# S and DP formed as rows in four column groups, and wider wq transfers, in a one-core attention and MLP gradient kernel

## Chip, cores and metric

The kernel runs on one NeuronCore of a Trainium2 chip. The core has a matrix engine (TensorE, PE in the profile; its weight loads are shown apart as PEld), a vector engine (DVE), an activation engine (ACT), GpSimd (POOL) and a queue engine (SP) that here issues nearly all transfers. The transfers themselves run on 16 DMA engines. Each engine works through its own queue in order; engines wait for each other through semaphores. The metric is the device time of one execution in microseconds (us), lower is better.

## Reference

One decode step and all its gradients. An attention block with 32 heads reads one query row against a cache of 4096 keys and values a head; a small MLP runs beside it, and a gate mixes the two. Cut to what matters:

```python
q = (x @ wq).reshape(32, 128)
scores = einsum("hd,hkd->hk", q, k_cache) * 128 ** -0.5
p = softmax(scores)
o = einsum("hk,hkd->hd", p, v_cache)
a = o.reshape(4096) @ wo
b = mish(x @ w1 + b1) @ w2
out = g * a + (1 - g) * b            # g = sigmoid(x . gate_w)
# returned: out, and the gradients of x, k_cache, v_cache, wq, wo, w1, b1, w2, gate_w
```

The caches are 32 x 4096 x 128 in bf16, so K and V are read once (2 x 33.6 MB) and dK and dV written once (the same). For a head, S is the row of 4096 scores. DP is the row of 4096 products of V with dO, the gradient of o for that head. p is softmax(S), and ds = p * (DP - D) with one number D a head. dV is the outer product of p and dO, dK that of ds and q.

## The kernel before

**Tiling.** The 4096 keys of a head lie as 128 partitions x J = 32 keys x 128 numbers, 1 MB (`Kn`, four buffers, and `Vn`, three). S and DP are kept as 128 partitions x 32, the same layout, in PSUM. The 32 heads run one after the other in groups of G = 4 heads; a group shares 512 columns of wq (`wq_p`, one transfer of 1.3 MB for two groups, in runs of 2048 B) and 512 rows of wo (`wo_g`).

**One head.** The order in the source is the order in each engine's queue. For head h:

- `v_tr` (four blocks, `tr_block`, L514 and L515): PE transposes V as f32 words into the PSUM tile `tr` (two buffers), ACT copies each block of 512 columns to `VT`. Between the blocks stand `dqo_mm` (L624), four f32 products of the head before on the weights `od_sb`, and `softmax` (L548, L550), which turns the diagonal `dgm` of the partition maxima into the head's maximum `negM`.
- `dk_out(h - 1)` (L581): DVE forms dK of the head before in the buffer `o_sb` (two instructions of 128 x 2048), and SP issues its store (L591).
- `exps` (L556): ACT takes the exponentials of S. `dP` (L522): PE forms DP with `cols_mm`, then DVE multiplies DP with them (`pj`, L562).
- `k_tr(h + 1)`: K of the next head is transposed to `KT` in four blocks, with `zd_mm` (L566, the sums over partitions of the exponentials and of `pj`) after the second block. DVE then makes p and ds (`probs`, L570 to L576) and dV (`dv_out`, L581).
- `scores(h + 1)`: S of the next head with `cols_mm` (L522), DVE takes its maximum over the 32 columns (`m`, L542), ACT makes `dgm` (L544).
- `dq_o` (L611): 16 products in four column groups of PE, K with ds and V with p, 512 columns each, into `od4`; `od_cp` (L618) copies it to `od_sb` on ACT.

`cols_mm` uses the transposed keys as weights: for each of 16 words and two halves of a word it loads 128 x 128 bf16 weights from T and multiplies them with a 32-column slice of `qz` (for S) or `doz` (for DP), a tile in which q or dO of the head stands in two columns between zeros. So S and DP take 32 weight loads and 32 products each, all summed in one 128 x 32 tile. T is one of `KT` and `VT`, one buffer each.

**Group work.** Around the heads of a group stand the steps for the neighbours: `g_q`, `g_do`, `g_dodiag`, `g_dobc`, `g_docol`, `g_dopair` prepare q and dO of the next group (`pair_cp`, L235, writes `qz` and `doz` in two DVE instructions), `f_diag`, `f_bc`, `f_dx`, `f_dwq`, `f_dwo` finish the gradients of the group before, `mlp_some` and `dw2_some` spread the MLP over the heads. `load_wqp` is called at the end of groups 0, 2 and 4 (and once at the start), `f_dwq_st` stores dwq after every second group.

**Queues.** SP issues loads and stores in program order: `load_k(h + 4)` and `load_v(h + 3)` after `od_cp(h)`, each store after its producer. The last stores are dV and dK of head 31 (L591), behind the small outputs `fin_rows`.

Of the kernel before, what the change touches and what calls it, by code (L numbers as in the profile page):

```python
# [16 lines left out]
def kernel(  # L17
# [24 lines left out]
    nc = tc.nc  # L42
# [71 lines left out]

    wqp = {}

    def load_wqp(k):
        wqp[k] = wts.tile([P, RC, 2 * GD], BF16, name="wq_p", tag="wq_p", bufs=2)
        for i in range(2):
            wqs[2 * k + i] = wqp[k][:, :, i * GD:(i + 1) * GD]  # L120
        nc.sync.dma_start(wqp[k][:], wq_v[:, :, 2 * k * GD:2 * (k + 1) * GD])

    def load_wo(g):
        wos[g] = wts.tile([P, G, D], BF16, name="wo_g", tag="wo_g")
# [58 lines left out]
    dx_parts = const.tile([P, RC, NG + 3], F32, name="dx_parts")  # L183

    p4b, ds4b = [], []
    qz = const.tile([P, G, 3 * J - 2], BF16, name="qz")
    doz = const.tile([P, G, 3 * J - 2], BF16, name="doz")
    nc.gpsimd.memset(qz[:], 0.0)
    nc.gpsimd.memset(doz[:], 0.0)
    for i in range(3):  # L190
        for lst, nm in ((p4b, "p4"), (ds4b, "ds4")):
            lst.append(const.tile([P, J * 4], BF16, name=f"{nm}{i}"))
# [3 lines left out]

    def g_new(g):
        groups[g] = dict(
            q_row=grp_sb.tile([P, GD], BF16, name="q_row", tag="q_row"),
            qs_row=grp_sb.tile([P, GD], BF16, name="qs_row", tag="qs_row"),  # L200
            do_row=grp_sb.tile([P, GD], BF16, name="do_row", tag="do_row"),
            do_col=grp_sb.tile([P, G], F32, name="do_col", tag="do_col"),
            dqo=grp_sb.tile([P, 2, G], F32, name="dqo", tag="dqo"),
        )
# [26 lines left out]
        return ps  # L231

    def pair_cp(z, ps):
        for par in range(2):
            nc.vector.tensor_tensor(z[:, :, J - 2 + par * J:J + par * J],  # L235
                                    ps[:, par, :].unsqueeze(2).to_broadcast([P, G, 2]),
                                    half[:].unsqueeze(1).to_broadcast([P, G, 2]), ALU.mult)

    def g_qcol(g):
        groups[g]["col"] = col_mm(groups[g]["q_row"])  # L240
# [13 lines left out]
    def g_do(g, hh):  # L254
        gp = groups[g]
        junk = small.tile([P, D], BF16, name="junk", tag="junk", bufs=1)
        nc.vector.scalar_tensor_tensor(junk[:], in0=wos[g][:, hh, :], scalar=1.0, in1=da_bc[:],  # L257
                                       op0=ALU.mult, op1=ALU.mult, accum_out=gp["do_col"][:, hh:hh + 1])

    def g_diag(src, sc, a, b):  # L260
        diag = grp_sb.tile([P, G, P], BF16, name="diag", tag="diag")
# [21 lines left out]
    def f_new(g):  # L283
        gp = groups[g]
        gp["o_bf"] = grp_sb.tile([P, G], BF16, name="o_bf", tag="o_bf")
        gp["dq_bc"] = grp_sb.tile([P, GD], BF16, name="dq_bc", tag="dq_bc")

    def f_diag(g, a=0, b=G):
        gp = groups[g]
# [87 lines left out]
        nc.vector.tensor_scalar(wqs[g][:, c, cs], groups[g]["dq_bc"][:, cs], x_col_f[:, c:c + 1], None, ALU.mult)  # L377

    def f_dwq_st(g):
        if g % 2:  # L380
            k = g // 2
            nc.sync.dma_start(dwq_v[:, :, 2 * k * GD:2 * (k + 1) * GD], wqp[k][:])

    def f_dwo(g, hh):
        nc.scalar.activation(wos[g][:, hh, :], da_bc[:], ACT.Copy, scale=groups[g]["o4"][:, hh:hh + 1])  # L385
# [124 lines left out]
    def tr_block(src, dst, c):  # L510
        tp = tr_ps.tile([P, TB // 2, P], F32, name="tr", tag="tr")
        words = src[:, c * TB:(c + 1) * TB, :].rearrange("p a b -> p (a b)").bitcast(F32)
        for t in range(TB // 2):
            nc.tensor.transpose(tp[:, t, :], words[:, t * P:(t + 1) * P], ident_f[:])  # L514
        nc.scalar.copy(dst[:, c * (TB // 2):(c + 1) * (TB // 2), :], tp[:])  # L515

    def cols_mm(out, T, z):
        Tb = T[:].rearrange("p c r -> p (c r)").bitcast(BF16).rearrange("p (c r a) -> p c r a", r=P, a=2)
        for c in range(J // 2):
            for par in range(2):  # L520
                a = J - 2 - 2 * c + par * J
                nc.tensor.matmul(out, lhsT=Tb[:, c, :, par], rhs=z[:, a:a + J],  # L522
                                 start=(c == 0 and par == 0), stop=(c == J // 2 - 1 and par == 1))

    def k_tr(h, c):
        if h < H:
            if c == 0:
                KT[h] = kvT.tile([P, J // 2, P], F32, name="KT", tag="KT")
            tr_block(kts[h], KT[h], c)

    def v_tr(h, c):
        if c == 0:
            VT[h] = kvT.tile([P, J // 2, P], F32, name="VT", tag="VT")
        tr_block(vts[h], VT[h], c)

    def scores(h):
        if h >= H:
            return
        S_ps[h] = s_ps.tile([P, J], F32, name="S", tag="S")
        cols_mm(S_ps[h][:], KT.pop(h), qz[:, h % G, :])  # L540
        m32 = small.tile([P, 1], F32, name="m32", tag="m32")
        nc.vector.reduce_max(m32[:], S_ps[h][:], axis=AX.X)  # L542
        dgms[h] = small.tile([P, P], F32, name="dgm", tag="dgm", bufs=1)
        nc.scalar.activation(dgms[h][:], ident_bf[:], ACT.Copy, scale=m32[:])  # L544

# [7 lines left out]
    def exps(h, negM):  # L553
        es[h] = small.tile([P, J], BF16, name="e_bf", tag="e_bf")
        zds[h] = small.tile([P, 2], F32, name="zd", tag="zd")
        nc.scalar.activation(es[h][:], S_ps.pop(h)[:], ACT.Exp, bias=negM[:], scale=scale, accum_out=zds[h][:, 0:1])  # L556

    def dP(h):
        DP_ps[h] = s_ps.tile([P, J], F32, name="DP", tag="DP")
        cols_mm(DP_ps[h][:], VT.pop(h), doz[:, h % G, :])  # L560
        pj = small.tile([P, J], F32, name="pj", tag="pj")
        nc.vector.scalar_tensor_tensor(pj[:], in0=DP_ps[h][:], scalar=1.0, in1=es[h][:],  # L562
                                       op0=ALU.mult, op1=ALU.mult, accum_out=zds[h][:, 1:2])

    def zd_mm(h, mx):
# [2 lines left out]
    def probs(h, mx):  # L568
        rz = small.tile([P, 1], F32, name="rz", tag="rz")
        nc.vector.reciprocal(rz[:], mx[:, P:P + 1])  # L570
        negD = small.tile([P, 1], F32, name="negD", tag="negD")
        nc.vector.tensor_scalar(negD[:], mx[:, P + 1:P + 2], rz[:], -1.0, ALU.mult, ALU.mult)
        p4s[h] = p4b[h % 3][:, 0:J * 4].rearrange("p (j t) -> p j t", t=4)
        nc.vector.tensor_scalar(p4s[h], es.pop(h)[:].unsqueeze(2).to_broadcast([P, J, 4]), rz[:], None, ALU.mult)
        ds4s[h] = ds4b[h % 3][:, 0:J * 4].rearrange("p (j t) -> p j t", t=4)
        nc.vector.scalar_tensor_tensor(ds4s[h], in0=DP_ps.pop(h)[:].unsqueeze(2).to_broadcast([P, J, 4]),  # L576
                                       scalar=negD[:], in1=p4s[h], op0=ALU.add, op1=ALU.mult)
        zds.pop(h)

# [13 lines left out]
    def dv_out(h):  # L593
        out_pair(h, dVv, p4s[h], groups[h // G]["do_row"])
# [10 lines left out]
    def dq_o(h):  # L605
        K, V = kts.pop(h), vts.pop(h)
        for r in range(J // 8):
            for c in range(4):
                N, c4 = (K, ds4b[h % 3]) if c < 2 else (V, p4b[h % 3])
                jb = 4 * (2 * r + c % 2)  # L610
                nc.tensor.matmul(od4[32 * c:32 * c + 4, :],  # L611
                                 lhsT=c4[:, 4 * jb:4 * jb + 16].rearrange("p (j t) -> p t j", t=4)[:, 0, :],
                                 rhs=N[:, jb:jb + 4, :].rearrange("p j d -> p (j d)"),
                                 start=(r == 0), stop=(r == J // 8 - 1))

    def od_cp(h):
        od_sb[h] = small.tile([P, 4, Dh], F32, name="od_sb", tag="od_sb", bufs=1)
        nc.scalar.copy(od_sb[h][:].rearrange("p j d -> p (j d)"), od4[:])  # L618

    def dqo_mm(h):  # L620
# [90 lines left out]
    for h in range(H - 1):  # L711
# [206 lines left out]
```

## Time and profile before

| | |
|---|---|
| median of 3 runs | 407.63 us (407.42 to 408.31) |
| profiled execution | 409.23 us, its span in the profile 407.4 us |
| moved by DMA | 164.76 MB, 404 GB/s on average |
| wq_p load | 4 transfers of 1280 KB |
| dwq store | 4 transfers of 1280 KB |
| K load, V load, dK and dV store | 32, 32 and 64 transfers of 1024 KB |
| weight loads of L522 | 2 x 1024, 100 and 97 ns |
| products of L522 | 2 x 1024, 180 and 177 ns, overlapping |
| o_sb, L581 | 128 instructions, 1217 ns each |
| ACT copies of T, L515 | 256, 585 and 588 ns each |

The page shows one execution taken by the hardware profiler, times in us unless marked ns. "Busy" is the time in which an engine had work in it; PE's matrix products are pipelined, so single products overlap and their ends are modelled. The rows of 40 digits cut the span in 40 slices and give the busy share of each in tenths; PEclk is the share of the full clock that PE was granted, DMA the mean share of the 16 DMA engines. The chain that ended last goes back from the last instruction, at each step to what released it. A line of a timeline gives the start, the time from the first to the last of the merged instructions, engine, source line, operation, the tile written and read, the count, and in brackets idle time before it with its releaser. In a line of waits stand the total, the number of waits and the longest. A line of stretches gives its length, then for PE, PEld, DVE, ACT and POOL the busy time and number of instructions, then the granted clock, the DMA share and GB/s.

### The profile page before, as it was taken

Reading aid. Unit: us, or ns where it says so; the run is one execution under the profiler, and the core shown is the slowest. Engines: PE = TensorE matmul, PEld = TensorE weight load, DVE = VectorE, ACT = ScalarE, POOL = GpSimd, SP = SyncE. Lnnn points to the kernel's source line nnn. Section 1 sums busy time; section 2 is a strip of 40 time slices with the busy share of each in tenths; the row PEclk is TensorE's granted clock in tenths of the full one; section 3 lists DMA queues with packets and bytes.
Section 4 is the critical chain, followed back from the end, with each engine's and each line's share of the span. In section 5 each row is a group of like instructions: output and inputs, shape, how many; then the busy total and the mean of one; then the engine's idle time right before and its main releaser. Section 6 shows DMA issues by size and latency. Waiting matters only on the chain.

```text
span 407.4 us, 10856 instructions
## 1 busy us (share of the span) xinstructions
PE 332.7 (82%) x4445; PEld 271.9 (67%) x4445; DVE 306.6 (75%) x845; ACT 232.6 (57%) x479; POOL 10.0 (2%) x25
## 2 busy tenths in 40 slices
PE   2698998889898998989898898879989798989600
PEld 1487776677686977877677678758777676877500
DVE  3646774797898587998999785666899987995640
ACT  2345556666476453765567666765776553776520
POOL 3000001000000000000000003000000000000000
PEclk9989999989898597999999896787999987899755
DMA  8999999999999999999999999999999999999883
GB/s 290 427 415 422 416 414 404 403 420 421 417 421 423 422 419 421 414 426 421 424 424 425 426 418 425 416 426 422 424 408 405 426 417 425 422 386 421 359 333 133
DMA packets 28695, 164.76 MB, mean 404 GB/s; under 512 B 2916, under 2 KB 3045, under 8 KB 12262
## 3 DMA queue, kind: packets, MB, share of 16 engines
q1 hardware_dynamic: 28338, 164.05, 97.8%
q8 instruction: 35, 0.57, 0.5%
q14 instruction: 14, 0.11, 0.1%
q0 software_dynamic: 256, 0.01, 0.0%
q10 hardware_dynamic: 52, 0.01, 0.0%
HBM read 82.03 MB, written 82.03 MB: 403 GB/s over the span
## 4 chain that ended last, share of the span: by engine, by line
DVE 44%; PE 34%; ACT 10%; issue 5%; DMA 2%; DVEq 0%; ACTq 0%; SPq 0%
DVE o_sb L581 22%; PE tr L514 15%; PE dqo_ps L624 7%; DVE junk L327 3%; PE DP L522 3%; ACT od_sb L618 2%; DVE junk L257 2%; DVE ds L576 2%; DMA wq_p<-in_A_wq_dram 2%; PE q_ps L210 2%; PE od L611 2%; PE mx L548 2%; ACT KT L515 2%; ACT VT L515 2%; ACT wo_g L385 2%
## 5 line engine op out<-in xcount | busy, mean ns | idle before, releaser
L515 ACT COPY VT<-tr 128x512 f32<-128x512 f32 x128 | 72.6, 585 | 43.3 <-PE tr L514 41.4
L514 PE MATMUL tr<-ident_f,Vn 128*128 128x128 f32 x512 | 90.2, 314 | 3.4 <-ACT VT L515 1.8
L515 ACT COPY KT<-tr 128x512 f32<-128x512 f32 x128 | 69.8, 588 | 39.4 <-PE tr L514 38.7
L514 PE MATMUL tr<-ident_f,Kn 128*128 128x128 f32 x512 | 78.6, 301 | 8.7 <-DMA Kn<-in_A_k_cache_dram 5.9
L514 PEld LDWEIGHTS tr<-ident_f,Vn 128*128 128x128 f32 x512 | 69.1, 166 | 15.0 <-ACT VT L515 7.3
L581 DVE TENSOR_TENSOR o_sb<-qs_row,ds 128x2048 bf16<-128x2048 bf16 x64 | 75.2, 1217 | 0.3 <-DMA out_dram<-o_sb 0.3
L581 DVE TENSOR_TENSOR o_sb<-do_row,p 128x2048 bf16<-128x2048 bf16 x64 | 75.2, 1217 | 0.0
L514 PEld LDWEIGHTS tr<-ident_f,Kn 128*128 128x128 f32 x512 | 61.3, 154 | 13.6 <-DVE ident_f L165 5.8
L544 ACT ACTIVATE dgm<-ident_bf,m 128x128 f32<-128x128 bf16 x32 | 12.8, 401 | 57.8 <-DVE m L542 48.6
L550 DVE TENSOR_REDUCE negM<-mx 128x1 f32<-128x128 f32 x32 | 9.3, 291 | 44.8 <-PE mx L548 34.0
L624 PE MATMUL dqo_ps<-sel,od_sb 128*128 128x2 f32 x256 | 37.2, 267 | 6.8 <-ACT od_sb L618 5.1
L624 PEld LDWEIGHTS dqo_ps<-sel,od_sb 128*128 128x128 f32 x256 | 35.5, 215 | 9.7 <-ACT od_sb L618 7.3
L522 PE MATMUL DP<-doz,VT 128*128 128x32 bf16 x1024 | 37.0, 180 | 2.3
L522 PEld LDWEIGHTS <-VT 128*128 128x128 bf16 x1024 | 34.0, 100 | 6.4 <-ACT VT L515 4.3
L522 PEld LDWEIGHTS <-KT 128*128 128x128 bf16 x1024 | 32.3, 97 | 6.0 <-ACT KT L515 3.2
L522 PE MATMUL S<-qz,KT 128*128 128x32 bf16 x1024 | 34.2, 177 | 1.9
L611 PE MATMUL od<-Kn,ds 128*4 128x512 bf16 x256 | 33.3, 382 | 0.0
L611 PE MATMUL od<-Vn,p 128*4 128x512 bf16 x256 | 33.3, 382 | 0.0
L257 DVE SCALAR_TENSOR_TENSOR junk<-wo_g,da_bc 128x640 bf16<-128x640 bf16 x32 | 26.3, 820 | 0.4
L385 ACT ACTIVATE wo_g<-da_bc,o 128x640 bf16<-128x640 bf16 x32 | 24.6, 820 | 0.0
L327 DVE SCALAR_TENSOR_TENSOR junk<-wq_p,dq_bc 128x512 bf16<-128x512 bf16 x35 | 24.0, 687 | 0.5
L618 ACT COPY od_sb<-od 128x512 f32<-128x512 f32 x32 | 18.2, 568 | 1.4 <-PE od L611 1.2
(171 smaller groups left out, 337.4 us busy)
## 6 DMA issues: line engine op xcount, KB each, us to landing
out_dram<-o_sb SPq DMA_DIRECT2D x64, 1024.0 KB, 15.1
Kn<-in_A_k_cache_dram SPq DMA_DIRECT2D x32, 1024.0 KB, 17.2
Vn<-in_A_v_cache_dram SPq DMA_DIRECT2D x32, 1024.0 KB, 17.9
wq_p<-in_A_wq_dram SPq DMA_DIRECT2D x4, 1280.0 KB, 14.7
wo_g<-in_A_wo_dram SPq DMA_DIRECT2D x8, 640.0 KB, 16.9
out_dram<-wo_g SPq DMA_DIRECT2D x8, 640.0 KB, 17.5
out_dram<-wq_p SPq DMA_DIRECT2D x4, 1280.0 KB, 16.3
w_sb<-in_B_w_dram SPq DMA_DIRECT2D x1, 2160.0 KB, 23.1
```

What stands on the lines that cost most here:

```text
L257: nc.vector.scalar_tensor_tensor(junk[:], in0=wos[g][:, hh, :], scalar=1.0, in1=da_bc[:], op0=ALU.mult, op1=ALU.mult, accum_out=gp["do_col ...
L327: nc.vector.scalar_tensor_tensor(junk[:, cs], in0=wqs[g][:, c, cs], scalar=1.0, in1=gp["dq_bc"][:, cs], op0=ALU.mult, op1=ALU.mult, accum_ ...
L385: nc.scalar.activation(wos[g][:, hh, :], da_bc[:], ACT.Copy, scale=groups[g]["o4"][:, hh:hh + 1])
L514: nc.tensor.transpose(tp[:, t, :], words[:, t * P:(t + 1) * P], ident_f[:])
L515: nc.scalar.copy(dst[:, c * (TB // 2):(c + 1) * (TB // 2), :], tp[:])
L522: nc.tensor.matmul(out, lhsT=Tb[:, c, :, par], rhs=z[:, a:a + J], start=(c == 0 and par == 0), stop=(c == J // 2 - 1 and par == 1))
L544: nc.scalar.activation(dgms[h][:], ident_bf[:], ACT.Copy, scale=m32[:])
L550: nc.vector.tensor_reduce(negM[:], mx[:, 0:P], axis=AX.X, op=ALU.max, negate=True)
L581: nc.vector.tensor_tensor(dst[:, a:b, :].rearrange("p j (k t) -> p j k t", t=4), row.rearrange("p (k t) -> p k t", t=4).unsqueeze(1).to_br ...
L611: nc.tensor.matmul(od4[32 * c:32 * c + 4, :], lhsT=c4[:, 4 * jb:4 * jb + 16].rearrange("p (j t) -> p t j", t=4)[:, 0, :], rhs=N[:, jb:jb + ...
L618: nc.scalar.copy(od_sb[h][:].rearrange("p j d -> p (j d)"), od4[:])
L624: nc.tensor.matmul(od_sb[h][:], lhsT=t[:, j, :], rhs=sel[:, :, j], start=(j == 0), stop=(j == 3))
```

## The change

S and DP are formed the other way round. Now q (or dO) is the weight, two columns of it, and the transposed keys are the moving side: `rows_mm` sends 512 columns of T through each of four column groups of PE, once for each half of a word, eight products in all. The result `row4` has two rows in each group. ACT copies it to `row_sb` (128 x 512 f32), and the new `cols_mm` turns it back into the 128 x 32 layout with four f32 products against a fixed selection `sel_s`. The two parts are separate calls in the head's order: `dp_rows` before and `dP` after the first block of `k_tr(h + 1)`; `s_rows(h + 1)` before and `scores(h + 1)` after `dq_o(h)`. S and DP share one PSUM tile `sdp`.

`KT` and `VT` share one buffer; `row_sb` shares its buffer with the old `od_sb`; `q_row`, `diag` and `dq_bc` have one buffer instead of two. `qz` and `doz` shrink to two columns a head, and `pair_cp` writes them in one instruction. wq of groups 2 to 5, and dwq of them, become one transfer each of 2.6 MB in runs of 4096 B; groups 0 and 1, and 6 and 7, stay as pairs, and share one buffer.

```diff
+    WQP = [(0, 2), (2, 6), (6, NG)]
     def load_wqp(k):
-        wqp[k] = wts.tile([P, RC, 2 * GD], BF16, name="wq_p", tag="wq_p", bufs=2)
-        for i in range(2):
-            wqs[2 * k + i] = wqp[k][:, :, i * GD:(i + 1) * GD]
-        nc.sync.dma_start(wqp[k][:], wq_v[:, :, 2 * k * GD:2 * (k + 1) * GD])
+        a, z = WQP[k]
+        wqp[k] = wts.tile([P, RC, (z - a) * GD], BF16, name="wq_p", tag=f"wq_{z - a}", bufs=1)
+        for g in range(a, z):
+            wqs[g] = wqp[k][:, :, (g - a) * GD:(g - a + 1) * GD]
+        nc.sync.dma_start(wqp[k][:], wq_v[:, :, a * GD:z * GD])
...
-    qz = const.tile([P, G, 3 * J - 2], BF16, name="qz")
-    doz = const.tile([P, G, 3 * J - 2], BF16, name="doz")
-    nc.gpsimd.memset(qz[:], 0.0)
-    nc.gpsimd.memset(doz[:], 0.0)
+    qz = const.tile([P, 2, G, 2], BF16, name="qz")
+    doz = const.tile([P, 2, G, 2], BF16, name="doz")
+    sel_s = const.tile([P, 4, J], F32, name="sel_s")
+    nc.gpsimd.memset(sel_s[:], 0.0)
+    for i in range(2):
+        nc.gpsimd.affine_select(
+            out=sel_s[:], in_=sel_s[:], compare_op=ALU.not_equal, fill=1.0,
+            base=-3 * i, pattern=[[-8, 4], [4, J]], channel_multiplier=-1,
+        )
...
-            q_row=grp_sb.tile([P, GD], BF16, name="q_row", tag="q_row"),
+            q_row=grp_sb.tile([P, GD], BF16, name="q_row", tag="q_row", bufs=1),
...
     def f_dwq_st(g):
-        if g % 2:
-            k = g // 2
-            nc.sync.dma_start(dwq_v[:, :, 2 * k * GD:2 * (k + 1) * GD], wqp[k][:])
+        for k, (a, z) in enumerate(WQP):
+            if g == z - 1:
+                nc.sync.dma_start(dwq_v[:, :, a * GD:z * GD], wqp[k][:])
...
-    def cols_mm(out, T, z):
-        Tb = T[:].rearrange("p c r -> p (c r)").bitcast(BF16).rearrange("p (c r a) -> p c r a", r=P, a=2)
-        for c in range(J // 2):
-            for par in range(2):
-                a = J - 2 - 2 * c + par * J
-                nc.tensor.matmul(out, lhsT=Tb[:, c, :, par], rhs=z[:, a:a + J],
-                                 start=(c == 0 and par == 0), stop=(c == J // 2 - 1 and par == 1))
+    def rows_mm(T, z, hh):
+        Tb = T[:].rearrange("p c r -> p (c r)").bitcast(BF16).rearrange("p (g n a) -> p g n a", g=4, a=2)
+        for par in range(2):
+            for c in range(4):
+                nc.tensor.matmul(row4[32 * c:32 * c + 2, :], lhsT=z[:, par, hh, :], rhs=Tb[:, c, :, par],
+                                 start=(par == 0), stop=(par == 1))
+        row_sb = small.tile([P, 4, P], F32, name="row_sb", tag="row_sb", bufs=1)
+        nc.scalar.copy(row_sb[:].rearrange("p c r -> p (c r)"), row4[:])
+        return row_sb
+
+    def cols_mm(out, row_sb):
+        for c in range(4):
+            nc.tensor.matmul(out, lhsT=row_sb[:, c, :], rhs=sel_s[:, c, :], start=(c == 0), stop=(c == 3))
...
+    s_rows(0)
+    g_dodiag(0)
     scores(0)
-    g_dodiag(0)
...
         exps(h, negM)
+        dp_rows(h)
+        k_tr(h + 1, 0)
         dP(h)
-        k_tr(h + 1, 0)
         k_tr(h + 1, 1)
...
         dv_out(h)
+        s_rows(h + 1)
+        dq_o(h)
         scores(h + 1)
-        dq_o(h)
         od_cp(h)
...
-            if g % 2 == 0 and g + 2 < NG:
-                load_wqp(g // 2 + 1)
+            if g in (0, 4):
+                load_wqp(g // 4 + 1)
```

More of the change, by code (lines that the diff above doesn't have):

```diff
@@ L115 @@
     wqp = {}
+    WQP = [(0, 2), (2, 6), (6, NG)]
+    assert NG == 8
     def load_wqp(k):
-        wqp[k] = wts.tile([P, RC, 2 * GD], BF16, name="wq_p", tag="wq_p", bufs=2)
-        for i in range(2):
-            wqs[2 * k + i] = wqp[k][:, :, i * GD:(i + 1) * GD]
-        nc.sync.dma_start(wqp[k][:], wq_v[:, :, 2 * k * GD:2 * (k + 1) * GD])
+        a, z = WQP[k]
[3 more added lines that the diff above has]
+        nc.sync.dma_start(wqp[k][:], wq_v[:, :, a * GD:z * GD])
     def load_wo(g):
@@ L233, in pair_cp @@
     def pair_cp(z, ps):
-        for par in range(2):
-            nc.vector.tensor_tensor(z[:, :, J - 2 + par * J:J + par * J],
-                                    ps[:, par, :].unsqueeze(2).to_broadcast([P, G, 2]),
-                                    half[:].unsqueeze(1).to_broadcast([P, G, 2]), ALU.mult)
+        nc.vector.tensor_tensor(z[:].rearrange("p a h j -> p (a h) j"),
+                                ps[:].rearrange("p a h -> p (a h)").unsqueeze(2).to_broadcast([P, 2 * G, 2]),
+                                half[:].unsqueeze(1).to_broadcast([P, 2 * G, 2]), ALU.mult)
     def g_qcol(g):
@@ L260, in g_diag @@
     def g_diag(src, sc, a, b):
-        diag = grp_sb.tile([P, G, P], BF16, name="diag", tag="diag")
+        diag = grp_sb.tile([P, G, P], BF16, name="diag", tag="diag", bufs=1)
         for hh in range(a, b):
@@ L274, in g_dodiag @@
         gp = groups[g]
-        gp["do_diag"] = grp_sb.tile([P, G, P], BF16, name="diag", tag="diag")
+        gp["do_diag"] = grp_sb.tile([P, G, P], BF16, name="diag", tag="diag", bufs=1)
         nc.vector.tensor_tensor(gp["do_diag"][:].rearrange("p h d -> p (h d)").rearrange("p (k t) -> p k t", t=4),
@@ L285, in f_new @@
         gp["o_bf"] = grp_sb.tile([P, G], BF16, name="o_bf", tag="o_bf")
-        gp["dq_bc"] = grp_sb.tile([P, GD], BF16, name="dq_bc", tag="dq_bc")
+        gp["dq_bc"] = grp_sb.tile([P, GD], BF16, name="dq_bc", tag="dq_bc", bufs=1)
     def f_diag(g, a=0, b=G):
@@ L515, in tr_block @@
         nc.scalar.copy(dst[:, c * (TB // 2):(c + 1) * (TB // 2), :], tp[:])
-    def cols_mm(out, T, z):
-        Tb = T[:].rearrange("p c r -> p (c r)").bitcast(BF16).rearrange("p (c r a) -> p c r a", r=P, a=2)
-        for c in range(J // 2):
-            for par in range(2):
-                a = J - 2 - 2 * c + par * J
-                nc.tensor.matmul(out, lhsT=Tb[:, c, :, par], rhs=z[:, a:a + J],
-                                 start=(c == 0 and par == 0), stop=(c == J // 2 - 1 and par == 1))
+    row4 = s_ps.tile([P, 4 * P], F32, name="row4", tag="row4")
+    nc.vector.memset(row4[:], 0.0)
+    sdp = s_ps.tile([P, 2, J], F32, name="sdp", tag="sdp")
+    def rows_mm(T, z, hh):
[10 more added lines that the diff above has]
+            nc.tensor.matmul(out, lhsT=row_sb[:, c, :], rhs=sel_s[:, c, :], start=(c == 0), stop=(c == 3))
     def k_tr(h, c):
@@ L527, in k_tr @@
             if c == 0:
-                KT[h] = kvT.tile([P, J // 2, P], F32, name="KT", tag="KT")
+                KT[h] = kvT.tile([P, J // 2, P], F32, name="KT", tag="T")
             tr_block(kts[h], KT[h], c)
@@ L532, in v_tr, with s_rows @@
         if c == 0:
-            VT[h] = kvT.tile([P, J // 2, P], F32, name="VT", tag="VT")
+            VT[h] = kvT.tile([P, J // 2, P], F32, name="VT", tag="T")
         tr_block(vts[h], VT[h], c)
+    rows_sb = {}
+    def s_rows(h):
+        if h < H:
+            rows_sb["S"] = rows_mm(KT.pop(h), qz, h % G)
     def scores(h):
@@ L538, in scores @@
             return
-        S_ps[h] = s_ps.tile([P, J], F32, name="S", tag="S")
-        cols_mm(S_ps[h][:], KT.pop(h), qz[:, h % G, :])
+        S_ps[h] = sdp[:, 0, :]
+        cols_mm(S_ps[h], rows_sb.pop("S"))
         m32 = small.tile([P, 1], F32, name="m32", tag="m32")
-        nc.vector.reduce_max(m32[:], S_ps[h][:], axis=AX.X)
+        nc.vector.reduce_max(m32[:], S_ps[h], axis=AX.X)
         dgms[h] = small.tile([P, P], F32, name="dgm", tag="dgm", bufs=1)
@@ L555, in exps, with dp_rows @@
         zds[h] = small.tile([P, 2], F32, name="zd", tag="zd")
-        nc.scalar.activation(es[h][:], S_ps.pop(h)[:], ACT.Exp, bias=negM[:], scale=scale, accum_out=zds[h][:, 0:1])
+        nc.scalar.activation(es[h][:], S_ps.pop(h), ACT.Exp, bias=negM[:], scale=scale, accum_out=zds[h][:, 0:1])
+    def dp_rows(h):
+        rows_sb["DP"] = rows_mm(VT.pop(h), doz, h % G)
     def dP(h):
-        DP_ps[h] = s_ps.tile([P, J], F32, name="DP", tag="DP")
-        cols_mm(DP_ps[h][:], VT.pop(h), doz[:, h % G, :])
+        DP_ps[h] = sdp[:, 1, :]
+        cols_mm(DP_ps[h], rows_sb.pop("DP"))
         pj = small.tile([P, J], F32, name="pj", tag="pj")
-        nc.vector.scalar_tensor_tensor(pj[:], in0=DP_ps[h][:], scalar=1.0, in1=es[h][:],
+        nc.vector.scalar_tensor_tensor(pj[:], in0=DP_ps[h], scalar=1.0, in1=es[h][:],
                                        op0=ALU.mult, op1=ALU.mult, accum_out=zds[h][:, 1:2])
@@ L575, in probs @@
         ds4s[h] = ds4b[h % 3][:, 0:J * 4].rearrange("p (j t) -> p j t", t=4)
-        nc.vector.scalar_tensor_tensor(ds4s[h], in0=DP_ps.pop(h)[:].unsqueeze(2).to_broadcast([P, J, 4]),
+        nc.vector.scalar_tensor_tensor(ds4s[h], in0=DP_ps.pop(h).unsqueeze(2).to_broadcast([P, J, 4]),
                                        scalar=negD[:], in1=p4s[h], op0=ALU.add, op1=ALU.mult)
@@ L616, in od_cp @@
     def od_cp(h):
-        od_sb[h] = small.tile([P, 4, Dh], F32, name="od_sb", tag="od_sb", bufs=1)
+        od_sb[h] = small.tile([P, 4, Dh], F32, name="row_sb", tag="row_sb", bufs=1)
         nc.scalar.copy(od_sb[h][:].rearrange("p j d -> p (j d)"), od4[:])
@@ L831 @@
     exps(h, negM)
+    dp_rows(h)
     dP(h)
```

## Prediction

> **What bounds the kernel now.** I read the page first (busy shares, clock and DMA slices, the chain), then the waits, then the timeline of one ordinary head, then busy time by stretches.
>
> ```profile
> PE 332.7 (82%) x4445; PEld 271.9 (67%) x4445; DVE 306.6 (75%) x845; ACT 232.6 (57%) x479; POOL 10.0 (2%) x25
> ...
> PEclk9989999989898597999999896787999987899755
> DMA  8999999999999999999999999999999999999883
> ...
> q8 instruction: 35, 0.57, 0.5%
> ...
> DVE 44%; PE 34%; ACT 10%; issue 5%; DMA 2%; DVEq 0%; ACTq 0%; SPq 0%
> ```
>
> Two things look like the bound. The 16 DMA engines are nine tenths busy or more from the second slice to the third last. But the chain that ended last is 88% DVE, PE and ACT, and 2% DMA. The waits decide between them:
>
> ```profile
> ACT dgm L544 <- DVE m L542: 48.6, 25, 2.5
> ...
> DVE negM L550 <- PE mx L548: 34.0, 17, 5.5
> ...
> DVE pj L562 <- PE DP L522: 6.8, 9, 2.2
> ...
> PE tr L514 <- DMA Kn<-in_A_k_cache_dram: 5.9, 1, 5.9
> ```
>
> The one large wait for a landing is the first K. After it the compute engines wait for each other. So each head is a closed loop of work that hands over from engine to engine, and DMA keeps up because its queue was filled at the start. Head 2, from its maximum m to the next head's:
>
> ```profile
> 39.95 0.18 DVE L542 TENSOR_REDUCE m<-S 128x1 f32<-128x32 f32 x1
> ...
> 40.53 0.57 ACT L618 COPY od_sb<-od 128x512 f32<-128x512 f32 x1
> ...
> 41.15 1.05 PE L624 MATMUL dqo_ps<-sel,od_sb 128*128 128x2 f32 x8 [0.72 <-ACT od_sb L618]
> ...
> 42.74 1.92 ACT L515 COPY VT<-tr 128x512 f32<-128x512 f32 x3 [1.15 <-PE tr L514]
> ...
> 43.87 1.21 PE L522 MATMUL DP<-doz,VT 128*128 128x32 bf16 x32
> ...
> 45.50 0.18 DVE L562 SCALAR_TENSOR_TENSOR pj<-DP,e_bf 128x32 f32<-128x32 f32 x1
> ...
> 46.99 1.07 ACT L515 COPY KT<-tr 128x512 f32<-128x512 f32 x2 [0.26 <-PE tr L514]
> ...
> 47.27 1.21 PE L522 MATMUL S<-qz,KT 128*128 128x32 bf16 x32
> 47.35 2.35 DVE L581 TENSOR_TENSOR o_sb<-do_row,p 128x2048 bf16<-128x2048 bf16 x2
> ...
> 48.41 0.38 PE L611 MATMUL od<-Kn,ds 128*4 128x512 bf16 x2
> ...
> 49.62 0.18 DVE L542 TENSOR_REDUCE m<-S 128x1 f32<-128x32 f32 x1
> ```
>
> V's last copy ends at 44.66, DP at 45.08, and pj follows at 45.50. K's last copy ends at 48.06, S at 48.48, and m follows at 49.62 behind the dV product. So 24 of the 32 products of each sum run while the last copy is made, and only 0.42 us stand behind it. The loop is 9.67 us. Read the same way in the timeline, the steps from m to m of heads 0 to 30 sum to 353.3 us, 11.4 us a head with the work of the groups in it.
>
> **The change, part by part.** *DP as rows.* Removed: 32 weight loads and products. Added, behind V's last copy: two rounds of four products, a copy of 512 columns by ACT, four f32 products (sel_s). Their nearest rows: od, also four column groups of 512 columns, starts a round every 0.21 us (48.41, 48.63, 48.85, 49.06); the od_sb copy is of the same size, 0.57; dqo, four f32 products with the same kind of weights, is 1.05 and starts 0.05 behind its copy. From V's last copy: 0.15 to the fourth group's first product (as DP now), 0.21 to its second, 0.50 to the copy (in head 31 od's last round starts at 380.70 and the copy at 381.20), 0.57 copy, 0.05, 1.05: DP ends 2.53 us behind V's copy instead of 0.42. pj follows 0.11 behind DP at the least; over heads 0 to 30 it now starts 0.45 behind on average. So pj comes 2.53 + 0.11 - 0.43 - 0.45 = 1.76 us later, 55 us over 31 heads; heads 14 and 26, whose pj is 1.2 and 2.2 us behind DP anyway, take less: 53. Queued behind: on ACT the copy stands ahead of K's four copies, and on PE sel_s's products ahead of K's second block of transposes. Following that queue, K's last copy ends 5.13 us behind V's instead of 3.40, which is the same 1.73, so both ways round the loop move together. zd then waits for that second block, 0.05 a head: 1.6.
>
> *S as rows.* The same detour behind K's last copy, but od's 16 products stand between rows and sel_s: 0.15 + 0.21 + four rounds of 0.21, 0.32 until the next work starts behind od's last round (49.06 to 49.38), 1.05: S ends 2.6 behind K's copy instead of 0.44. m now starts 1.16 behind S on average, 0.11 at the least: 2.6 + 0.11 - 0.44 - 1.16 = 1.11 a head, 34 over 31. What waits for m is dgm on ACT, od_sb queued behind it there, then dqo and mx on PE, negM and dK on DVE: nothing that could hide it. Head 31 has only the DP detour: 2.
>
> PE also stands still 0.32 us behind od's last round, where it goes from four column groups back to whole products. DP as rows brings two more such changes a head, 0.64 us; both lie inside the wait for ACT's copy (0.50 + 0.57), so I count nothing.
>
> *Unknown prices.* Rows read T two bytes out of four, which no product here does as the moving side: a round between 0.21 (od) and 0.42 (twice od's), 0 to 26 us over 62 detours with two rounds each; I take 0.21, since the weight loads of L522 read T with that step now, 100 ns, and those of L269's ones without one are 100 ns too. The f32 products are 32 columns wide: between 0.6 (a block of four f32 transposes) and 1.2 (DP's 32 products); I take dqo's 1.05, the same weights. The low end takes away 28 us, the high end adds 9.
>
> *Transfers.* wq and dwq of groups 2 to 5, 5.24 MB, go in runs of 4096 B. In the stretch 388.5 to 390.5, where mostly 2048 B runs move, DMA makes 385 GB/s, in 200 to 220, K, V and outputs, 425. So they take 13.6 us now and 12.3 at the best: 0 to 1.3, I take 0.65. PE's instructions arrive as 35 packets (q8), one for 254 of its 8890 records; it has 2048 fewer, 8 packets of 16 KB, 0.3 us. Neither counts while the loop paces; if DMA did, 1 us.
>
> *At no cost.* One buffer for q_row, diag and dq_bc: each is written at one head of four and last read a head or more before the next write. T shared by K and V: K's copy stands behind ACT's row copy, which has waited for V's rows. row_sb shared with od_sb: od_sb stands behind dgm, which needs S. Without these covers each would add up to 0.57 a head. sel_s replaces two POOL fills before 5 us and is first used after 16. One instead of two products per qz or doz: 0.12 x 16, -2.
>
> *The end.* The last o_sb is ready at 391.6, its store and the one before are issued at 394.32 and 395.07, and the span ends at 407.4. The first K, issued at 0.74, was there at 5.87, and a further 1 MB at 425 GB/s takes 2.5: two such transfers alone 7.6 us, to 401.9. The other 5 us are earlier stores that DMA is behind with, and a longer loop leaves it none: -5.
>
> Sum: 53 + 34 + 2 + 2 - 2 - 5 = +84. The profiled execution took 409.23 us (span 407.4), so 493; the runs' median is 1.6 lower: **491 us**.
>
> **Rivals.** *More half speed on PE.*
>
> ```profile
> 154.20:157.60 3.40, 1.64 (x22) 0.83 (x14) 3.37 (x7) 1.65 (x4) 0.00 (x0) 1.00 1.02 424
> 157.60:164.40 6.80, 6.76 (x62) 6.53 (x62) 4.55 (x16) 2.24 (x6) 0.00 (x0) 0.50 1.01 422
> ```
>
> A stretch with PE busy 1.64 of 3.40 us is followed by 6.8 us at clock 0.50. Heads 12, 20 and 28, each with such a stretch, take 12.7 us, heads 16 and 24 of the same kind 10.5: 2.2. Eighteen slow windows of 3.4 us between 24 and 380 cost so about 20. The loop gains some 2 us of PE idleness a head; twice the windows: 511. Against it: no single new gap exceeds 0.7 us. The Trainium skill, "TensorE: Matmul & The Clock Gate", Part 1, says that an idle window of about 3.4 us halves the clock; the trace agrees with the length, but its windows were half busy.
> *Changes between whole and grouped products unhidden*: the 0.64 us x 31 = 20 from above, 511. For it, the 0.32 us appears behind every od; against it, the copy covers it. The Trainium skill, "TensorEngine Tiling (Array Packing)", section Key Properties, says that a change of tiling mode drains TensorE, which would apply at each of them; the 0.32 us agrees, and no run here shows how much of it a wait can hide.
> *Cheaper detours.* f32 products at 0.6: 491 - 28 = 463; with the slow windows gone too, 443.
> *No overlap of the four groups.* Each round 0.84: 1.26 more a detour, 78 us, 569. od's rows, two starting at once, speak against it.
> *The other side: DMA paces.* If the heads are in truth held back by transfers, through buffers that come free late, the detours fill idle time and the transfers decide: 407.6 - 1 = 406.6. The DMA slices speak for it; the waits, the chain and the even 9.6 us of the plain heads against. It decides only while the added time a head stays under some 0.16 us, the 5 us of the end over 31 heads. That the rows are not built is excluded: the built program's PE queue has them.
>
> **How the numbers follow.** Forecast (478 to 502) 0.48; half speed 0.14; changes unhidden 0.05; cheaper 0.22; no overlap 0.03; DMA paces 0.08. The range 445 to 520 takes in all but the last two, with half speed up to twice and a half of today's. 0.2%, 0.8 us, is what runs of this kernel can tell apart; DMA pacing gives -0.25%, so I split its 0.08 into 0.06 faster and 0.02 same; slower 0.92.
>
> **What would show it.** Right: m to m of a plain head near 12.4 us; DP ending some 2.5 us behind V's last copy, S 2.6 behind K's; DMA slices down to about eight tenths; PE waiting for ACT's row_sb. Wrong: plain heads still near 9.7; sel_s's four products well under 1 us; PEclk all nines (cheaper) or many fives (half speed); DMA still full.

## The result and the profile after

The changed kernel took 482.53 us, the median of six runs (479.19 to 485.22), beside 407.93 for the kernel before (407.34 to 408.88): a ratio of 1.183, with a 95% interval of 1.178 to 1.189. It is 75 us slower. The forecast was 491, the range 445 to 520. The profiled execution took 481.38 us, with a span of 479.4; the span before was 407.4, so the two traces differ by 72.0 us. Below, medians and ranges are of all runs of a kernel, and ratios are of its fast runs alone.

From the page after, engines, clock and DMA slices, instruction packets and the chain:

```profile
PE 411.5 (86%) x3421; PEld 283.7 (59%) x3421; DVE 309.3 (65%) x830; ACT 274.2 (57%) x543; POOL 10.1 (2%) x26
...
PEclk9998899988989699988989899977999889898865
DMA  8999987999899997989989987999679899999737
...
q8 instruction: 27, 0.44, 0.3%
...
PE 66%; ACT 19%; DVE 7%; issue 4%; DMA 2%; DVEq 0%; ACTq 0%; SPq 0%
```

PE has 1024 products fewer and is busy 79 us longer: the 32 bf16 products of a sum took 1.21 us, most of it under a copy, and the four f32 products alone take 1.08 in the head below. DMA, full before, now has slices at 6 to 8 tenths, and DVE has gone from the chain (44% to 7%): its dV product no longer decides when the next maximum starts. The 27 instruction packets are the 35 less 8 of the forecast.

The waits after (time in all, how often, the longest):

```profile
DVE pj L589 <- PE sdp L541: 70.3, 32, 4.6
ACT dgm L568 <- DVE m L566: 47.6, 32, 2.4
...
ACT row_sb L536 <- PE row L533: 41.1, 64, 1.1
...
PEld sdp L541 <- ACT row_sb L536: 25.4, 60, 1.3
DVE m L566 <- PE sdp L541: 20.1, 25, 1.1
```

pj's wait for DP has gone from 6.8 to 70.3 us; 41.1 and 25.4 are the two hand-overs inside the detour, PE to ACT and back; and m, which used to wait behind the dV product, now waits for S. An ordinary head, the 30th, shows it in order of time (the timeline; start, duration, engine and line; what ended the idle time in brackets):

```profile
421.72 0.19 DVE L566 TENSOR_REDUCE m<-sdp 128x1 f32<-128x32 f32 x1 [0.67 <-PE sdp L541]
...
425.60 1.07 ACT L523 COPY VT<-tr 128x512 f32<-128x512 f32 x2 [0.26 <-PE tr L522]
...
425.98 1.36 PE L533 MATMUL row<-VT,doz 128*2 128x512 bf16 x8
...
427.27 0.66 PE L522 MATMUL tr<-ident_f,Kn 128*128 128x128 f32 x4
427.43 0.58 ACT L536 COPY row_sb<-row 128x512 f32<-128x512 f32 x1 [0.48 <-PE row L533]
...
428.07 1.08 PE L541 MATMUL sdp<-sel_s,row_sb 128*128 128x32 f32 x8
428.87 0.50 PEld L522 LDWEIGHTS tr<-ident_f,Kn 128*128 128x128 f32 x4
...
429.26 0.19 DVE L589 SCALAR_TENSOR_TENSOR pj<-sdp,e_bf 128x32 f32<-128x32 f32 x1 [1.71 <-PE sdp L541]
...
430.43 1.15 ACT L523 COPY KT<-tr 128x512 f32<-128x512 f32 x2 [0.18 <-PE tr L522]
...
432.33 0.58 ACT L536 COPY row_sb<-row 128x512 f32<-128x512 f32 x1 [0.76 <-PE row L533]
...
433.03 1.08 PE L541 MATMUL sdp<-sel_s,row_sb 128*128 128x32 f32 x8
...
434.15 0.19 DVE L566 TENSOR_REDUCE m<-sdp 128x1 f32<-128x32 f32 x1 [0.90 <-PE sdp L541]
```

V's last copy ends at 426.67, DP at 429.15, 2.48 behind it, and pj follows in 0.11. K's last copy ends at 431.58, S at 434.11, 2.53 behind it, and m follows in 0.04. From m to m it is 12.43 us; the same head before took 9.65.

### The profile page after: what moved, and what is told of

The parts are those of the page before. It is cut to its first block, busy times and chain, and to the rows that moved or that the text cites. A ratio compares the mean times of both kernels' runs of the same rounds, so it can differ in the third digit from the quotient of the medians.

```text
span 479.4 us, 8859 instructions
## 1 busy us (share of the span) xinstructions
PE 411.5 (86%) x3421; PEld 283.7 (59%) x3421; DVE 309.3 (65%) x830; ACT 274.2 (57%) x543; POOL 10.1 (2%) x26
## 4 chain that ended last, share of the span: by engine, by line
PE 66%; ACT 19%; DVE 7%; issue 4%; DMA 2%; DVEq 0%; ACTq 0%; SPq 0%
PE tr L522 21%; PE sdp L541 14%; PE row L533 10%; PE dqo_ps L651 6%; PE od L638 6%; ACT VT L523 5%; ACT KT L523 4%; ACT row_sb L536 3%; ACT row_sb L645 3%; DMA wq_p<-in_A_wq_dram 2%; PE mx L572 2%; PE mx L593 1%; ACT wo_g L393 1%; DVE m L566 1%; DVE junk L265 1%
## 5 line engine op out<-in xcount | busy, mean ns | idle before, releaser
L522 PEld LDWEIGHTS tr<-ident_f,Vn 128*128 128x128 f32 x512 | 75.4, 176 | 8.9 <-ACT VT L523 5.9
L541 PEld LDWEIGHTS sdp<-sel_s,row_sb 128*128 128x128 f32 x512 | 62.9, 193 | 27.4 <-ACT row_sb L536 25.4
L541 PE MATMUL sdp<-sel_s,row_sb 128*128 128x32 f32 x512 | 69.7, 280 | 5.5 <-ACT row_sb L536 1.9
L536 ACT COPY row_sb<-row 128x512 f32<-128x512 f32 x64 | 37.5, 585 | 41.1 <-PE row L533 41.1
L589 DVE SCALAR_TENSOR_TENSOR pj<-sdp,e_bf 128x32 f32<-128x32 f32 x32 | 6.1, 192 | 70.3 <-PE sdp L541 70.3
L533 PE MATMUL row<-VT,doz 128*2 128x512 bf16 x256 | 41.8, 471 | 5.7 <-ACT VT L523 4.9
L651 PE MATMUL dqo_ps<-sel,row_sb 128*128 128x2 f32 x256 | 35.3, 260 | 8.2 <-ACT row_sb L645 6.5
L533 PE MATMUL row<-KT,qz 128*2 128x512 bf16 x256 | 36.2, 395 | 5.1 <-ACT KT L523 3.0
L638 PE MATMUL od<-Vn,p 128*4 128x512 bf16 x256 | 40.3, 383 | 0.0
L651 PEld LDWEIGHTS dqo_ps<-sel,row_sb 128*128 128x128 f32 x256 | 33.5, 204 | 11.4 <-ACT row_sb L645 8.9
```

The lines of the kernel that those rows point to most:

```text
L533: nc.tensor.matmul(row4[32 * c:32 * c + 2, :], lhsT=z[:, par, hh, :], rhs=Tb[:, c, :, par], start=(par == 0), stop=(par == 1))
L536: nc.scalar.copy(row_sb[:].rearrange("p c r -> p (c r)"), row4[:])
L541: nc.tensor.matmul(out, lhsT=row_sb[:, c, :], rhs=sel_s[:, c, :], start=(c == 0), stop=(c == 3))
L638: nc.tensor.matmul(od4[32 * c:32 * c + 4, :], lhsT=c4[:, 4 * jb:4 * jb + 16].rearrange("p (j t) -> p t j", t=4)[:, 0, :], rhs=N[:, jb:jb + ...
L651: nc.tensor.matmul(od_sb[h][:], lhsT=t[:, j, :], rhs=sel[:, :, j], start=(j == 0), stop=(j == 3))
```

## The experiments

Twelve kernels, in three steps: the change taken apart, the kernel before moved and relieved, and then what the first step left open. In the diffs, "-" is the kernel named as the start of each, and only the lines that matter are shown. The traces of the main ones, read as above (us; "run" is the median of all runs, the rest comes from one trace: "heads" is the sum of the steps from m to m, the next three are medians over heads 0 to 30; "half" counts the 3.41 us windows at half clock in these heads):

```
                        run    heads  DP-V   S-K   K-V   half
before                 407.8   353.3  0.42  0.42  3.41    19
changed                482.5   426.7  2.47  2.54  4.90    21
DP alone as rows       456.2   406.5  2.47  0.62  4.90    22
S alone as rows        471.7   416.9  1.29  2.54  4.27    33
S alone, own tile      431.1   382.1  0.42  2.54  3.41    21
rows only              485.7   429.9  2.47  2.54  4.90    23
rows only, own buffers 487.6   427.3  2.47  2.54  4.90    22
bf16 sel               429.0   379.4  1.66  1.73  4.10    17
DP from the old row    483.6   431.6  1.67  2.55  4.64    30
```

DP-V: from the end of V's last copy to DP's end; S-K: from K's last copy to S's end; K-V: between the two last copies.

**DP alone as rows** (from the changed kernel; `cols_direct` is `cols_mm` of the kernel before, and `qz` has its old layout).

```diff
-        cols_mm(S_ps[h], rows_sb.pop("S"))
+        cols_direct(S_ps[h], KT.pop(h), qz[:, h % G, :])
...
-        s_rows(h + 1)
-        dq_o(h)
         scores(h + 1)
+        dq_o(h)
```

> The changed kernel with DP alone as rows; S is summed by its 32 products as before. By the detours (each step behind the last copy lies on the loop): pj comes 1.85 us later behind V, K's last copy 1.5, and m goes on waiting for the dV product, which follows pj; so the heads grow by about 1.8 us, 56 in all, head 31 by 3 to 4, and the end shrinks by 6 to 7: 408 + 54 = 462, and a plain head takes 11.5. By PE's work (its busy time grew by 79 us, the span by 72, so the added products alone set the time): half of the added work is gone, 447 here as with S alone. By the transfers or shared buffers (they are all still in): the loss stays near 75, 482.

Measured: 456.16 us (454.84 to 459.0), ratio 1.119 (1.114 to 1.124). The heads are 53.2 us longer, head 31 by 3.7, the end behind the last o_sb shorter by 7.3. That is nearer to the detour's account (462) than to PE's work divided evenly (447) or to the transfers (482); PE's work is taken up again at the end of the old row's experiment. The sum of the forecast had 53 for this part. The trace is of a run of 459.0, 2.8 above the median.

**S alone as rows.** The mirror image: DP from VT by 32 products, its sums in the tile `sdp` that it shares with S.

> The changed kernel with S alone as rows; DP is summed by its 32 products as before. By the detours: S ends 2.1 us later behind K's copy, 1.16 of which m waited anyway for the dV product; 1.0 us a head, 31, head 0 by 2, the end -5: 408 + 28 = 436, a plain head 10.7. By PE's work: 447, as with DP alone. By the transfers or shared buffers: 482.

Measured: 471.65 (470.9 to 473.53), ratio 1.157 (1.154 to 1.160): a miss by 36 us, and more than S and DP together leave for S (482.5 - 456.2 = 26). The timeline of its third head has what no theory had named:

```profile
50.77 0.59 ACT L530 COPY VT<-tr 128x512 f32<-128x512 f32 x1 [0.27 <-PE tr L529]
51.25 0.29 ACT L595 ACTIVATE e_bf<-sdp,negM 128x32 bf16<-128x32 f32 x1
51.43 0.20 ACT L595 ACTIVATION_READ_ACCUMULATOR e_bf<-sdp,negM 128x1 f32 x1
51.69 0.95 PE L555 MATMUL sdp<-doz,VT 128*128 128x32 bf16 x32 [0.95 <-ACT e_bf L595]
```

and its waits the sum of it:

```profile
PE sdp L555 <- ACT e_bf L595: 30.5, 32, 1.0
```

DP's first product waits until the exponential has read S. The two use different columns of one tile. In the kernel before, with two tiles, 24 of DP's 32 products run while V's last copy is made; here all 32 stand behind the exponential, which ACT does after that copy. The Trainium skill, "PSUM — Partial Sum Buffer", section "PSUM bank collisions raise a hardware error", says that the compiler's scheduler adds a dependency between accesses of different engines to one bank and quarter of the partitions, whatever the columns. The 0.95 us here agree with it, but no run shows whether this rule put the wait in. The changed kernel shares the tile too, at no cost: its products wait for ACT's copy of the row, which ends at least 1.1 us behind the exponential in every head, and its list of waits has none of them for the exponential.

**S alone, DP in a tile apart from S.**

```diff
-        mx = s_ps.tile([P, P + 2], F32, name="mx", tag="mx")
+        mx = s_ps.tile([P, P + 2 + J], F32, name="mx", tag="mx")
+        DP_ps[h] = mx[:, P + 2:P + 2 + J]
...
-        DP_ps[h] = sdp[:, 1, :]
```

> S alone as rows again, with DP's sums in the PSUM tile of mx instead of the tile that S has. S alone as rows ran 471.7 where 436 was expected; its trace shows DP's first product waiting for the exponential to have read S from the shared tile, 0.95 us a head and 30.5 in all, and 33 windows at half clock in the heads where the kernel before has 19. If that wait is the cause and brought the windows with it: 436 to 441, DP 0.4 behind V's copy again. If the wait is one part and the windows another: 441 to 448, with the windows still near 33. If S's detour itself costs more than 1.0 a head: above 455.

Measured: 431.13 (428.09 to 432.51), ratio 1.056 (1.051 to 1.060). Only DP's tile differs, so the shared tile was the cause of the excess, and the windows went back with it (33 to 21). Its third head:

```profile
47.24 1.21 PE L555 MATMUL mx<-doz,VT 128*128 128x32 bf16 x32
...
47.44 0.59 ACT L530 COPY VT<-tr 128x512 f32<-128x512 f32 x1
47.92 0.29 ACT L596 ACTIVATE e_bf<-sdp,negM 128x32 bf16<-128x32 f32 x1
```

DP's products start before V's last copy again and end 0.42 behind it, at 48.45. S's detour alone costs 28.8 us over the heads, DP's alone 53.2: 82.0, where the two together cost 73.4. The medians hide this overlap. They give 48.4 us for DP alone and 23.4 for S alone, 71.8 of the 74.6 of both; that this comes so near is chance, since each of the two counts the some 7.3 us that are saved at the end, and both together save them once.

**Rows only**, wq and dwq as before (from the changed kernel: `load_wqp`, `f_dwq_st` and the call that loads are those of the kernel before).

> The changed kernel with wq and dwq moved as before (pairs of groups, 2048 B runs); S and DP as rows, the tiles with one buffer and the shared ones stay. By the detours: the loop paces and DMA has room, so within 1 us of the changed kernel, 482. By the transfers (a 2.6 MB transfer that holds the queue): several us below it, 470 to 478.

Measured: 485.69 (480.44 to 488.17), ratio 1.185 (1.176 to 1.194), an interval that holds the changed kernel's. So no part of the loss that these runs can tell comes from the transfers, and none is given back by them.

**Rows only, with buffers of their own.**

```diff
-            VT[h] = kvT.tile([P, J // 2, P], F32, name="VT", tag="T")
+            VT[h] = kvT.tile([P, J // 2, P], F32, name="VT", tag="VT")
...
-        od_sb[h] = small.tile([P, 4, Dh], F32, name="row_sb", tag="row_sb", bufs=1)
+        od_sb[h] = small.tile([P, 4, Dh], F32, name="od_sb", tag="od_sb", bufs=1)
...
-            q_row=grp_sb.tile([P, GD], BF16, name="q_row", tag="q_row", bufs=1),
+            q_row=grp_sb.tile([P, GD], BF16, name="q_row", tag="q_row"),
```

> The rows alone (wq and dwq in pairs of groups as before) with separate T for K and V, a tile of its own for od_sb, and two buffers again for q_row and dq_bc; diag keeps one. If the covers hold (V's rows are read before K's copy, S before od_sb): as with shared tiles, 483 to 486. If a shared buffer holds the copies back: up to 0.57 a head for each, 450 to 475.

Measured: 487.56 (482.08 to 491.27), ratio 1.198 (1.192 to 1.204): nothing is gained. DP ends as far behind V's copy and S behind K's as with shared tiles (2.47 and 2.54), so the covers named for them hold.

**The transfers without the rows** (from the kernel before: the 4096 B runs, the single buffers, and KT and VT with one tag).

> The kernel before with the transfers of 4096 B runs, the tiles with one buffer, and one T for K and V; S and DP as columns. By the detours: these edits cost nothing while the loop paces, and the end may gain up to 1.3 us: 406.6 to 408. By the transfers or shared buffers: a good part of the loss of 75 is here, over 415.

Measured: 407.96 (406.6 to 410.97), ratio 1.0006 (0.9983 to 1.0029): as the account by the detours has it, no difference that can be told.

**sel_s in bf16** (from the changed kernel).

```diff
-    sel_s = const.tile([P, 4, J], F32, name="sel_s", tag="sel_s")
+    sel_s = const.tile([P, 4, J], BF16, name="sel_s", tag="sel_s")
...
-        row_sb = small.tile([P, 4, P], F32, name="row_sb", tag="row_sb", bufs=1)
+        row_sb = small.tile([P, 4, P], BF16, name="row_bf", tag="row_bf", bufs=1)
```

> The changed kernel with the copy of the rows and sel_s in bf16, so that S and DP are of lower precision (od_sb has its own tile). It prices the four f32 products behind each copy, 1.05 us of the detour, eight records for four products. If a pass costs what it costs now, four passes take 0.53: 0.5 less a detour, 31 us over 62: 451. If the passes get shorter too, 0.25: DP's detour gives 0.8, S's only the 0.63 until the dV product sets m again, 44: 438. If the detour were set by the copy and its hand-overs, and the products lay beside them: within 5 us of the changed kernel.

Measured: 429.03 (427.71 to 431.54), ratio 1.053 (1.048 to 1.057), below the lowest expectation. From the timeline of its 30th head:

```profile
382.32 0.58 ACT L536 CAST row_bf<-row 128x512 bf16<-128x512 f32 x1 [0.48 <-PE row L533]
...
382.96 0.27 PE L541 MATMUL sdp<-sel_s,row_bf 128*128 128x32 bf16 x4
383.05 0.42 PEld L522 LDWEIGHTS tr<-ident_f,Kn 128*128 128x128 f32 x4
...
383.33 0.19 DVE L589 SCALAR_TENSOR_TENSOR pj<-sdp,e_bf 128x32 f32<-128x32 f32 x1 [0.90 <-PE sdp L541]
```

The four products end 0.27 after the first starts, where the f32 ones need 1.08, and the next block's weights load 0.09 after that start, where they had 0.80 to wait; its first product stands 0.11 behind instead of 0.91. The copy to bf16 costs the same 0.58. The heads are 47.3 us shorter than the changed kernel's 426.7, and 0.81 a detour is 50 over 62 of them. So some two thirds of what the heads lost (47.3 of 73.4) is the price of f32 in those products, four windows at half clock fewer (17 to 21) included; the rest is left for the rows, ACT's copy and the hand-overs, which no run here takes apart. The expectation of 438 for this case let the dV product set m again and so credited S's detour with only 0.63; both got shorter by 0.81.

**DP from the old row** (from rows only).

```diff
-        cols_mm(DP_ps[h], rows_sb.pop("DP"))
+        cols_mm(DP_ps[h], rows_sb["DP"])
+        rows_sb["DP"] = rows_sb.pop("DP_new")
...
         dp_rows(h)
+        dP(h)
         k_tr(h + 1, 0)
-        dP(h)
```

> The rows alone, but DP's four f32 products read the row copy of the head before, and stand right behind the row products instead of behind K's first block of transposes; od_sb has its own tile, row_sb three buffers. So DP is that of the head before and ds, dK and dq with it; the work on each engine is the same. If DP's detour is a chain of hand-overs (rows, copy, products): pj comes 0.6 us earlier, K's chain 0.4, the step is then set by S and shrinks by about 0.45: 14 us, 471. If PE's work alone sets the time: 483 to 486. If the copy's wait were the whole of the loss: 0.7 a head and more, below 462.

Measured: 483.57 (478.63 to 492.79), ratio 1.181 (1.175 to 1.188): no gain, which by the time alone speaks for PE's work. Its trace shows why the time says little. DP ends 0.8 earlier behind V, K's last copy 0.26, S sets m, and the heads without a half-clock window are shorter by that much (the twelfth 12.63 instead of 12.89). DP's products now also wait for the exponential, 18.0 us in all, so the chain was not shortened by all that the order could give. Over 31 heads the 0.26 are 8 us; but 30 windows at half clock stand where rows only has 23. What one costs can be read in the changed kernel from two heads of the same kind, busy time by stretch from m to m (columns: us, busy time and instructions of PE, PEld, DVE, ACT, POOL, granted clock, DMA share, GB/s):

```profile
201.73:215.26 13.53, 12.54 (x114) 9.23 (x114) 9.91 (x26) 8.41 (x16) 0.00 (x0) 0.87 0.86 355
255.14:267.58 12.44, 11.47 (x114) 8.12 (x114) 9.82 (x26) 8.21 (x16) 0.00 (x0) 1.00 0.90 352
```

The same 114 products take 1.1 us more at a clock of 0.87. At that price seven more windows cost about the 8 us that the shorter chain gave.

Is it the chain, then, or PE's work? The 447 expected of PE's work for DP alone and for S alone took its added time to divide evenly, which it does not. Over heads 0 to 30 PE is busy for 312.6 us in the kernel before, 386.0 in the changed one, 358.5 with DP alone and 344.9 with S alone in a tile apart. That is 73, 46 and 32 us more, where the heads take 73, 53 and 29 more; so 456 and 431 speak only against an even division. What shows that hand-overs count beyond PE's work are heads with the same products. The twelfth takes 12.24 us with S alone and 11.38 with DP in a tile apart, with PE busy for 10.80 and 10.78; it takes 12.89 in rows only and 12.63 with the old row, with PE busy for 11.91 and 11.86. But PE stands still for only 1.0 us of that head in rows only, and of the 30th head for 0.7 us before the change and 1.0 after it. So the chain runs mostly through PE: most of what the rows add is time in which PE is busy on it, the f32 products above all, and time in which it waits is the smaller part. The traces do not divide this further, since the ends of PE's products are modelled.

**m early** (from the kernel before: `out_pair` takes a function that it calls between its two products).

```diff
-        dv_out(h)
-        scores(h + 1)
+        dv_out(h, lambda: scores(h + 1))
         dq_o(h)
```

> The kernel before with m (and the scaled diagonal behind it on ACT) issued between the two halves of the dV product; nothing else. If the loop paces, m starts about 1.0 us earlier a head, up to 31 us over the heads, until the transfers decide: 164.6 MB at 425 GB/s are 387 us, with the 6 us before the first K and 4 to 8 at the end 397 to 402. If DMA paces the kernel before, the earlier m only waits elsewhere: 407 to 408.

Measured: 408.33 (407.49 to 409.21), ratio 1.0006 (0.9990 to 1.0021). The time is that of the rival, DMA. Its waits show landings that the kernel before (0.3 and 0.8 us) hardly waits for:

```profile
DVE o_sb L581 <- DMA out_dram<-o_sb: 8.2, 4, 4.5
...
PE tr L514 <- DMA Vn<-in_A_v_cache_dram: 3.5, 4, 1.6
```

The second and third heads do get shorter, 9.60 to 9.02 and 9.67 to 9.07, but by 0.6, not by the 1.0 or so that m stands closer to S; and negM then follows m after 3.5 us instead of 3.0. It waits for mx, whose products stand in PE's queue behind dqo's, and these wait for ACT's copy of od, which now starts 1.01 us behind the second head's m instead of 0.58. So about half of what m gains is lost again before negM.

**No dwq stores** (from the kernel before: the transfer in `f_dwq_st` is left out) **and m early without them.**

> The kernel before without the stores of dwq, so that dwq is not in the output; its work on the engines stays. 5.24 MB less, 12 to 13.6 us of DMA. If the loop paces: the heads stay at 353 us, and only the 15.8 us behind the last o_sb shrink, to some 8.5 as in the changed kernel: 400 to 403. If DMA paces the heads too: 394 to 396.

> The kernel before with m between the halves of the dV product and without the stores of dwq, so that dwq is not in the output. m early alone gained nothing (408.3), and its trace shows waits for landings that the kernel before lacks (o_sb's buffers 8.2 us, V 3.5). If DMA took over there, the 12 to 13.6 us that the stores take come off in full: 395 to 397, against 399.6 without the stores alone. If m early gains nothing for another reason: 399 to 400, as without the stores alone.

Measured: 399.61 (395.61 to 401.61), ratio 0.977 (0.973 to 0.981), and 396.17 (395.42 to 396.4), ratio 0.971 (0.969 to 0.973). Without the stores the kernel before gains 8.2 of their 12 to 13.6 us, and in its trace, of a run of 397.57, 6.5 at the end (15.8 to 9.3) and 4.8 in the heads, which also have 16 half-clock windows instead of 19. With m early, they come off in full, 12.2. So the kernel before was paced by its loop, with DMA only a few us behind it. With DMA relieved, an early m is worth some 3.4 us by the medians (heads 348.5 and 346.1): that much DMA took from it. The rest of the up to 31 us expected of it did not come even so.

**m early with the transfers**, both from the kernel before.

> The kernel before with m between the halves of the dV product and the transfers of 4096 B runs, the single buffers and the shared T. If m early leaves DMA as the bound, the transfers' 1.3 us count in full: 1.0 to 1.5 below m early alone. If the loop still paces: the same as m early alone.

Measured: 406.70 (406.06 to 408.8), ratio 0.9972 (0.9955 to 0.9989): 1.6 us below m early alone, the only version here with all outputs that beats the kernel before, by 0.3%. The longer runs show a gain once DMA is the bound; without the early m none could be told, where up to 0.7 us would lie inside the interval.

## Why the prediction was right

The direction held, and the mechanism in the main: the two detours stand where they were expected, at the length that was expected. The size came within 9 us. Term by term, from the two traces (the forecast's 84 against 72.0):

```
                      forecast   measured
heads, DP             53 + 1.6     53.2   (DP alone)
heads, S                 34        20.2   (73.4 for both, less 53.2)
pair_cp                  -2        in the above
head 0                    -        +2.1   (first m at 20.81 instead of 18.67)
head 31                  +2        +3.8   (m to the last o_sb)
the end                  -5        -7.3   (last o_sb to the end of the span)
```

The traces are single runs, that of DP alone 2.8 us above its median, so 53.2 and 20.2 are good to some 3 us.

- *DP's detour*: forecast 2.53 behind V's copy, measured 2.47 (median) in the changed kernel and the same with DP alone. Each piece was priced from a neighbour: od's rounds for the rows, od_sb for the copy, dqo for the f32 products, and each was near. For the rows this was in part luck. The second product of the fourth group starts 0.22 behind the first (426.95 and 426.73), so reading two bytes out of four costs nothing here. But the reason given for it was misread: L269's weight loads do not take 100 ns, eight of the 17 take 181 and eight 95 to 104.
- *S's detour*: forecast 2.6 behind K's copy, measured 2.54. The term was still 14 us too large, and the step that failed is the one that let K's last copy move by the same 1.73 as pj, "so both ways round the loop move together". It moved by 1.49 (3.41 to 4.90). The forecast took dqo's 1.05 both as the time to the result and as the time that PE is taken. The first is right, 1.08. But the next block's weights start 0.80 behind the first product (428.87 against 428.07). With both chains changed, K's last copy stands 2.32 behind pj on average instead of 2.75, which over 31 heads is 13 us, nearly the whole excess. With S alone K's last copy keeps its distance to pj (2.82), and S then costs 28.8 of the 34.
- *The credit for m*: S was charged only what it exceeds m's wait for the dV product. That held: m now starts 0.04 behind S, and the dV product, which used to end as m started, ends 0.63 before it on average.
- *Transfers, shared and single buffers, at no cost*: shown by the transfers alone (407.96 and 407.81) and by the rows with their own buffers.
- *The end*: DMA caught up as forecast, 7.3 instead of 5 us. Head 31 was forecast too short by 1.8 and head 0's S left out, 2.1: S's detour there lies on the path to the first m, though S alone in a tile apart adds only 1.1 there (19.81). Head 31 has 14.2 us at half clock instead of 8.7.

Of the rivals, *DMA paces* is out with a ratio of 1.18, but came closer to the truth about the kernel before than its chance of 0.08 says: m early and the runs without the dwq stores show the two limits a few us apart. *More half speed*: 21 windows instead of 19 in the heads, some 2 us; it did not decide here, but it did eat the gain of the old row. The "some 2 us of PE idleness a head" that the forecast feared did not come: in the 30th head PE is idle for 0.7 us before and 1.0 after. *Changes unhidden* and *no overlap*: a detour would have been longer than the 2.5 that it is, DP's by up to 0.64 or each by 1.26. The 0.32 is there behind the rows (426.95 to 427.27), but what follows it on PE are transposes, which run while ACT's copy is awaited. *Cheaper detours*: the f32 products cost what dqo does.

## What to carry to other kernels

A sum moved behind a copy costs the whole chain from that copy to its result: of the 32 products that were replaced, 24 ran under the copy. Of what took their place, the last products of the rows, a second copy and four f32 products all stood behind it. Price such a detour from its nearest neighbours twice, as the time to its result and as the time that its engine is taken, and follow both chains. Where two sums are put into one PSUM tile, look for the reader of the first that the writer of the second will now wait for, and for what hides that wait.

## What was not expected of the hardware

Four f32 products of 128 rows and 32 columns hold PE for 0.80 us until the next weights load, 0.91 until the next block's first product, and 1.08 to their own end; in bf16 it is 0.09, 0.11 and 0.27. From bf16 to f32 the time until PE is free for the next block grew eight- to ninefold, the time to the result fourfold.

The number of half-clock windows varies between kernels with nearly the same work: 13 and 14 in two of the three with m early, 16 to 23 in most, 30 and 33 in the two where DP's products wait for the exponential (in the old row's trace too, 18.0 us in all). The Trainium skill, "TensorE: Matmul & The Clock Gate", Part 1, says that the window of 3413 ns runs freely and that what a kernel meets of it varies from run to run; the length agrees, 3.413 us in every trace. What in those two kernels brings ten more windows stays open.
